# Another fixed order for the attention and gate stages of a fused attention and mixture kernel

## The chip, the cores and the metric

The kernel runs on one core of a Trainium2 chip. The metric is device time in microseconds (us) of one execution; the runs of a kernel are given with their median. The engines are TensorE (PE in the rows, with PEld for its weight loads), VectorE (DVE), ScalarE (ACT), GpSimd (POOL) and SyncE (SP), which issues the DMAs here. Each engine works its own queue in order.

## The reference

Attention over 2 batches, 8 heads, 576 positions of width 64: a softmax over the keys within 3 positions, plus a softmax of averaged queries on averaged keys (factor 4) whose result is repeated four times. Its output is a matrix of 1152 tokens by 512. A gated layer and a mixture of eight experts follow:

```python
def _moe_ref(x, w_gate, w_val, w_out):
    g = x @ w_gate
    silu = g * (1.0 / (1.0 + np.exp(-g)))
    val = x @ w_val
    return silu * val @ w_out

def _moe2_ref(x, w_gate, w1, w2):
    logits = x @ w_gate
    P = np.exp(logits - logits.max())
    for _ in range(8):                      # rows and columns in turn
        ...
    for e in range(E):
        h = np.maximum(x @ w1[e], 0.0)
        out += P[:, e:e + 1] * (h @ w2[e])
```

## The kernel before, in words

Matrices are split into a high and a low half of 16 bits, so that a product is three matmuls for each block of depth (mm3, L219). The program has three stages: attention together with the preparation of the gate weights, the gate products, and from the output products on the experts. The first two follow one table, PLAN, which is read from left to right; each entry is a step and the number of its pair of heads (0 to 7) or of its block of 128 gate columns (0 to 11, in hexadecimal). Inside them every engine's queue keeps the order in which the table issued its instructions. Behind the bar in PLAN the attention's PSUM banks are closed and the late gate products begin. Behind the table stands act_split, and then a scheduler orders the rest.

Steps of a pair of heads: K, Q, Z and W are loads. kd and qd add four positions (DVE, or POOL through qt: qe L492, qd L499). s0, s1 and s2 are scores (TensorE), m0 to m2 their maxima (DVE L536, L537), e0 to e2 exponentials with sums (ACT). r makes the reciprocals of the sums (DVE L557, L558), and ha and hb multiply by them (POOL L563, L568, tile ex), so ha and hb wait for r. px, py and pv add values (POOL L504, L508, L515, tiles vt and vdz, or DVE L513 alone). t are transposes and c their copies (ACT), o the products with the values, w and j the join (ACT, DVE L625), u and l the high and low half of the result (ACT, DVE L639, tile xhl).

Steps of a gate block: gR is its load, ga to gd its conversion from 64 bits (gb L247 or L245, gB L250, gc L253, gd L256, all DVE; ga ACT), ge its maximum (ACT L286), gp and gq or a POOL reduction spread it, gm makes the scale, gh and gl the two halves (ACT L306, DVE L310). Blocks 0 to 2 have their first 512 tokens multiplied early (y0, y1, with ya to yd behind them); all other products are late ones: zp is the product for the gate, zs its SiLU (ACT L692), zq the product for the value, zv their product (DVE L694), zj its maximum. The first digit of a z step is the chunk of tokens, 0 for the first 512 and 1 for the other 640. Late products share two PSUM pairs: the third product waits until the first one's SiLU has read its pair. Steps beginning with w prepare the output weights. sa, sg, sb and sp split the gate result of chunk 0 into halves (ACT L211, DVE L212, three blocks to an sp), in the order in which the blocks' zp steps stood; the output products (TensorE, tile wo) of chunk 0 start behind them and read blocks 0 to 11 in that order, into the same two PSUM pairs.

FILL gives a number of products that nobody reads, of a constant tile (L131, tile warm), to be issued into a bank ahead of a step's own products.

Of the kernel before, what the change touches and what calls it, by code (L numbers as in the profile page):

```python
# [56 lines left out]
PLAN = """
K0 Q0 K1 Q1 K2 Q2 Z0 W0 W1 Z1 W2 kd0 qd0 s00 kd1 s10 m00 s20 e00 m10 qe1 s01 m20 K3 Q3 e10 qd1 kd2 W3
s11 m01 e20 qd2 s21 s02 e01 m11 K4 Q4 r0 gR0 m21 s12 ha0 e11 m02 pv1 s22 hb0 e02 m12 t0 pv0 e21 m22 c0
r1 kd3 e12 ha1 o0 qe3 e22 xg0 pv2 Z2 K5 w0 hb1 Q5 kd4 gR1 qd3 s03 j0 W4 qe4 r2 t1 xm0 m03 ha2 s13 e03  # L60
qd4 xp0 m13 s23 hb2 c1 xr0 xu0 ga0 o1 m23 u0 kd5 e13 t2 gb0 Z3 K6 l0 Q6 qe5 c2 pv3 W5 s04 w1 gB0 e23 s14
qd5 j1 gc0 u1 s24 ga1 o2 r3 m04 px4 m14 e04 ha3 m24 gd0 w2 e14 hb3 j2 ge0 l1 t3 qe6 kd6 e24 s05 gR2 W6
gb1 c3 Z4 qd6 gp0 K7 r4 s15 Q7 py4 gq0 m05 u2 W7 ha4 gm0 o3 e05 m15 l2 s25 gh0 pv4 pv5 hb4 e15 m25 t4
gl0 w3 e25 s06 px6 j3 c4 py6 s16 r5 gB1 ga2 ha5 m06 o4 kd7 u3 hb5 m16 e06 s26 gc1 t5 w4 e16 qe7 m26 xg1
j4 c5 pv6 gd1 s07 e26 px7 xm1 s17 ge1 l3 qd7 m07 xp1 py7 r6 gR3 gp1 e07 m17 s27 Z5 ha6 Z6 xr1 gq1 y00
xu1 e17 hb6 m27 gb2 tu0 u4 gm1 t6 gB2 ya0 l4 gh1 y10 yb0 c6 gc2 gl1 e27 o5 gd2 ga3 y01 pv7 r7 w5 ge2 yc0
ha7 j5 gR4 gb3 u5 gp2 Z7 hb7 y11 yd0 ya1 gq2 tl0 lb0 yj0 gm2 yb1 gh2 gB3 t7 yc1 gl2 o6 c7 yd1 y02 gc3 w6
ga4 l5 yj1 j6 o7 ya2 gd3 u6 y12 yb2 ge3 l6 gb4 w7 gR5 yc2 j7 gp3 yd2 u7 gB4 yj2 l7 gq3 gc4 | zp10 gm3
gd4 gh3 ge4 gl3 zp12 zs10 gq4 gR6 ga5 gm4 gh4 gb5 zq10 zs12 gB5 gl4 gc5 zq12 zv10 ga6 gd5 zj10 gb6 ge5
zp14 zv12 gq5 gR7 gB6 zj12 gm5 gc6 gh5 zp04 gd6 zs14 gl5 ge6 zp11 zs04 gq6 wR0 ga7 gm6 gh6 gb7 zp03 zs11  # L70
gl6 gB7 gc7 zp16 zs03 gd7 wa0 wb0 ge7 wB0 zq11 zs16 wc0 gq7 gR8 gm7 wd0 zq03 we0 zv11 gh7 wm0 wR1 zj11
zp06 gl7 wh0 zv03 ga8 wl0 zp05 zj03 gb8 zs06 gB8 wa1 zq14 gc8 zs05 wb1 gd8 wB1 ge8 zp13 zv14 wc1 gq8 gR9
zj14 gm8 wd1 gh8 zq04 zs13 gl8 we1 zp15 zv04 wR2 wm1 zj04 ga9 wh1 zp08 gb9 zs15 wl1 gB9 zp17 zs08 gc9
wa2 gd9 wb2 ge9 zq13 wB2 wc2 zs17 gq9 gRa wd2 zq17 gm9 we2 zv13 gh9 wm2 wR3 zj13 gl9 zq15 wh2 zv17 gaa
wl2 zj17 gba zp09 zv15 wa3 gBa zq05 zj15 gca zs09 wb3 gda zp19 zv05 gea wB3 zj05 wc3 gqa gRb gma zq16
zs19 wd3 gha we3 gla zp07 zv16 wR4 wm3 zj16 wh3 zq09 zs07 wl3 gab zp18 gbb wa4 zv09 gBb zj09 wb4 zp0a
gcb zs18 wB4 gdb zq18 zs0a wc4 geb wd4 gqb wR5 we4 gmb zq07 zv18 ghb wm4 zj18 glb zq0a wh4 zv07 wl4 zj07
wa5 zq06 zv0a wb5 zj0a wB5 zp0b wc5 zv06 wd5 zj06 zp1a zs0b we5 wm5 wh5 zq19 zs1a wl5 zq0b zv19 zj19
zq08 zv0b zj0b zp1b zv08 zj08 sa0 sg0 zq1a zs1b sb0 sp0 zq1b sp1 zv1a sp2 zj1a zv1b sp3 zj1b
"""  # L80
# [951 lines left out]
```

## Time and profile before

| what | value |
|---|---|
| median of 3 runs | 1006.35 us (1005.7 to 1007.02) |
| the profiled execution | 1003.09 us, span 1001.3 us |
| TensorE busy | 987.3 us, 99% of the span |
| DVE busy | 752.3 us, 75% |
| ACT busy | 439.0 us, 44% |
| POOL busy | 61.7 us, 6% |
| the start of the output products | 216.08 us |

The share of busy time is a mean over stages with different limits. A row of a timeline gives its start, its duration, engine, source line, operation and tiles (out<-in), and in brackets the idle time of the engine ahead of it with what ended it. The end of a matmul is modelled, so a busy TensorE is not one at its peak.

### The profile page before, as it was taken

How to read it: one execution, taken by the hardware profiler on the slowest of the kernel's cores; microseconds unless marked ns; L12 is line 12 of the kernel's file. 1: busy time of each engine (PE TensorE's matmuls, PEld its weight loads, DVE VectorE, ACT ScalarE, POOL GpSimd, SP SyncE). 2: the span in 40 equal slices, each digit the busy share in tenths (PEclk: the TensorE clock that was granted, in tenths of full speed). 3: DMA queues.
4: the chain of work that ended last, by engine and by line, in shares of the span. 5: the costliest groups of instructions: out<-in, count | busy, mean ns of one | idle time of the engine just before them, and what ended most of it. 6: DMA issues, size and time to landing. Idle time of an engine off the chain costs nothing.

```text
span 1001.3 us, 16401 instructions
## 1 busy us (share of the span) xinstructions
PE 987.3 (99%) x6592; PEld 619.3 (62%) x6596; DVE 752.3 (75%) x1532; ACT 439.0 (44%) x913; POOL 61.7 (6%) x80
## 2 busy tenths in 40 slices
...
GB/s 306 225 113 140 149 114 159 126 1 1 85 1 2 85 84 43 43 89 39 43 56 72 1 43 89 39 43 49 79 1 43 84 44 43 42 44 1 1 43 52
DMA packets 12987, 67.95 MB, mean 68 GB/s; under 512 B 1456, under 2 KB 1840, under 8 KB 6512
## 3 DMA queue, kind: packets, MB, share of 16 engines
...
q8 instruction: 51, 0.84, 0.4%
...
## 4 chain that ended last, share of the span: by engine, by line
PE 90%; DVE 7%; ACT 1%; DMA 1%; issue 1%; DVEq 0%; ACTq 0%
PE y L219 37%; PE p L219 32%; PE gv L219 11%; PE wo L219 7%; DMA v<-in_vd 1%; DVE s L536 1%; DVE xhl L639 1%; DVE cvg L256 1%; DVE cvg L253 1%; DVE ahl L212 0%; PE lt L748 0%; DVE x L625 0%; PE pw L131 0%; ACT ex L547 0%; DVE vdz L513 0%
## 5 line engine op out<-in xcount | busy, mean ns | idle before, releaser
L219 PE MATMUL y<-w,hhl 128*128 128x512 f16 (+1 forms) x1752 | 395.7, 376 | 0.0
L219 PE MATMUL p<-bop,w 128*128 128x320 f16 (+1 forms) x2688 | 353.5, 286 | 0.6 <-ACT s L917 0.4
L219 PEld LDWEIGHTS <-w 128*128 128x128 f16 x2688 | 262.9, 98 | 90.3 <-issue 2.0
L219 PEld LDWEIGHTS <-hhl 128*128 128x128 f16 x1752 | 171.5, 98 | 178.9
L928 ACT ACTIVATE hhl<-h 128x640 f16<-128x640 f32 (+1 forms) x128 | 82.7, 675 | 158.6 <-DVE h L900 158.6
L219 PE MATMUL gv<-xhl,gv 128*128 128x320 f16 (+1 forms) x864 | 142.1, 326 | 2.8 <-ACT act L692 1.1
L959 DVE SCALAR_TENSOR_TENSOR acc<-y,pe,acc 128x512 f32<-128x512 f32 (+1 forms) x64 | 47.3, 740 | 101.3 <-PE y L219 100.5
L211 ACT ACTIVATE w<-r,s_w 128x256 f16<-128x256 f32 (+1 forms) x96 | 71.2, 783 | 117.7 <-PE y L219 86.3
L219 PEld LDWEIGHTS <-gv 128*128 128x128 f16 x864 | 84.1, 98 | 58.8 <-issue 3.6
L929 DVE SCALAR_TENSOR_TENSOR hhl<-h,hhl 128x640 f16<-128x640 f32 (+1 forms) x128 | 93.9, 753 | 17.4 <-ACT hhl L928 16.4
L900 DVE SCALAR_TENSOR_TENSOR h<-p,u 128x256 f32<-128x256 f32 (+1 forms) x192 | 84.8, 452 | 19.4 <-PE p L219 13.9
L212 DVE SCALAR_TENSOR_TENSOR w<-r,s_w,w 128x256 f16<-128x256 f32 (+1 forms) x96 | 78.2, 834 | 16.8 <-ACT w L211 16.7
L219 PE MATMUL wo<-ahl,wo 128*128 128x320 f16 (+1 forms) x408 | 70.0, 326 | 0.0
L219 PEld LDWEIGHTS <-wo 128*128 128x128 f16 x432 | 42.0, 98 | 30.3 <-issue 1.7
L900 DVE SCALAR_TENSOR_TENSOR u<-p,u 128x320 f32<-128x320 f32 (+1 forms) x128 | 57.5, 449 | 4.2 <-PE p L219 3.4
L211 ACT ACTIVATE w<-cmb,s_w 128x512 f16<-128x512 f32 x64 | 43.0, 710 | 37.0 <-DVE cmb L384 35.0
L917 ACT ACTIVATE s<-p 128x256 f32<-128x256 f32 (+1 forms) x64 | 25.4, 396 | 54.9 <-PE p L219 54.8
L187 DVE TENSOR_REDUCE mxw<-r 128x1 f32<-128x1024 f32 x32 | 37.4, 1213 | 14.2 <-DMA r<-in_w 14.2
L212 DVE SCALAR_TENSOR_TENSOR w<-cmb,s_w,w 128x512 f16<-128x512 f32 x64 | 46.3, 743 | 0.0
L404 ACT ACTIVATE j<-r 128x1024 f16<-128x1024 f32 x32 | 33.5, 1047 | 26.9 <-DMA r<-in_w 24.1
...
L900 DVE SCALAR_TENSOR_TENSOR u<-p,s 128x256 f32<-128x256 f32 (+1 forms) x64 | 28.9, 451 | 3.9 <-PE p L219 3.9
...
## 6 DMA issues: line engine op xcount, KB each, us to landing
...
```

The source lines that it names most:

```text
L187: V.tensor_reduce(o, i, axis=axis, op=ALU.max, apply_absolute_value=True)
L211: return (A.activation(hi, src, AF.Copy, scale=s), V.scalar_tensor_tensor(lo, src, s, hi, op0=ALU.mult, op1=ALU.subtract))
L212: V.scalar_tensor_tensor(lo, src, s, hi, op0=ALU.mult, op1=ALU.subtract))
L219: T.matmul(ps, lhsT=wf(i, k), rhs=xf(j, k), start=n == 0, stop=n == 3 * nk - 1)
L253: V.scalar_tensor_tensor(o, hi, 0xC0000000, o, op0=ALU.bitwise_and, op1=ALU.bitwise_or)
L256: V.scalar_tensor_tensor(o, lo, 29, o, op0=ALU.logical_shift_right, op1=ALU.bitwise_or)
L404: A.activation(junk, t[:, 2 * j:2 * j + 2].rearrange("p a n -> p (a n)"), AF.Abs, accum_out=mx[:, 2 * i + j:2 * i + j + 1])
L900: V.scalar_tensor_tensor(o, ps, HSC, u, op0=ALU.mult, op1=ALU.add)
L917: A.activation(s1, p1, AF.Copy, scale=HSC)
L928: ra = A.activation(t[:, 0], h, AF.Relu)
L929: rv = V.scalar_tensor_tensor(t[:, 1], h, 0.0, t[:, 0], op0=ALU.max, op1=ALU.subtract)
L959: V.scalar_tensor_tensor(acc[t][:, ds], ps, p[:, t:t + 1], acc[t][:, ds], op0=ALU.mult, op1=ALU.add)
```

## The change

PLAN is another permutation of the same 562 steps, with the bar at the same place (305 steps ahead of it), and FILL has other numbers, 25 in sum where it had 21.

```diff
-FILL = {"s00": 3, "o0": 2, "o1": 1, "t3": 12, "t4": 3}
+FILL = {"s00": 3, "o0": 8, "t3": 8, "t4": 6}
 PLAN = """
...
-r1 kd3 e12 ha1 o0 qe3 e22 xg0 pv2 Z2 K5 w0 hb1 Q5 kd4 gR1 qd3 s03 j0 W4 qe4 r2 t1 xm0 m03 ha2 s13 e03
+m22 r1 e12 qe3 o0 ha1 e22 xg0 kd4 Z2 K5 qd3 pv2 w0 Q5 hb1 gR1 s03 r2 W4 qe4 j0 t1 xm0 m03 ha2 xp0 e03
...
```

The late products stand in this order before, zp10 zp12 zq10 zq12 zp14 zp04 zp11 zp03 zp16 zq11 zq03 zp06 zp05 zq14 zp13 zq04 zp15 zp08 zp17, and in this order now, zp10 zp12 zp11 zq12 zp14 zq10 zp04 zp03 zq14 zq03 zp06 zp16 zq11 zp05 zp13 zp17 zq04; the last three are zp1b zq1a zq1b in both. Block 6 is first read by zp16 before and by zp06 now, block 7 by zp17 in both. The reduction pv0 on DVE stood behind m12 and now stands ahead of m21.

POOL's queue from the addition of pair 4's values to the second share of pair 4. In the names, the digit behind ex, rs, qt, qd and vt is the pair. Before:

```order
L504 TENSOR_TENSOR vt4_619<-v44_415 72x256
L563 TENSOR_TENSOR ex3_448<-ex3_448,rs3_614 128x640
L568 TENSOR_TENSOR ex3_448<-ex3_448,rs3_614 96x432
L492 TENSOR_TENSOR qt6_673<-q6_541 128x576
L499 TENSOR_TENSOR qd6_698<-qt6_673 128x288
L508 TENSOR_TENSOR vt4_619<-v44_415 72x256
L563 TENSOR_TENSOR ex4_623<-ex4_623,rs4_704 128x640
L515 TENSOR_TENSOR vdz0_110<-vt4_619 72x256
L568 TENSOR_TENSOR ex4_623<-ex4_623,rs4_704 96x432
```

And of the changed kernel:

```order
L563 TENSOR_TENSOR ex3_449<-ex3_449,rs3_615 128x640
L568 TENSOR_TENSOR ex3_449<-ex3_449,rs3_615 96x432
L504 TENSOR_TENSOR vt4_670<-v44_420 72x256
L492 TENSOR_TENSOR qt6_685<-q6_561 128x576
L508 TENSOR_TENSOR vt4_670<-v44_420 72x256
L499 TENSOR_TENSOR qd6_727<-qt6_685 128x288
L515 TENSOR_TENSOR vdz0_110<-vt4_670 72x256
L563 TENSOR_TENSOR ex4_583<-ex4_583,rs4_742 128x640
L568 TENSOR_TENSOR ex4_583<-ex4_583,rs4_742 96x432
```

The first vt of pair 4 moved from ahead of the shares of pair 3 to behind them, the second one to ahead of qd6, and vdz0 to ahead of the shares of pair 4.

DVE's queue around the sums of pair 4 (rs4), which release ex4 on POOL, and the low half of pair 2 (xhl). Before:

```order
L557 TENSOR_REDUCE rs4_704<-sts0_112 128x16
L558 RECIPROCAL rs4_704<-rs4_704 128x16
L194 TENSOR_REDUCE gr_gv0_717<-sm0_700 128x1
L536 TENSOR_REDUCE s5_0_680<-s5_0_680 128x5
L537 TENSOR_SCALAR stb1_115<-s5_0_680 128x5
L180 TENSOR_SCALAR u_gv0_725<-gr_gv0_717 128x1
L181 TENSOR_SCALAR u_gv0_725<-u_gv0_725 128x1
L182 TENSOR_SCALAR s_gv0_726<-u_gv0_725 128x1
L183 TENSOR_SCALAR i_gv0_727<-u_gv0_725 128x1
L536 TENSOR_REDUCE s5_1_707<-s5_1_707 128x5
L537 TENSOR_SCALAR stb1_115<-s5_1_707 128x5
L639 SCALAR_TENSOR_TENSOR xhl_126<-x12_641,s_x10_476,xhl_126 128x512
```

And of the changed kernel:

```order
L536 TENSOR_REDUCE s5_0_674<-s5_0_674 128x5
L537 TENSOR_SCALAR stb1_115<-s5_0_674 128x5
L194 TENSOR_REDUCE gr_gv0_716<-sm0_697 128x1
L180 TENSOR_SCALAR u_gv0_718<-gr_gv0_716 128x1
L181 TENSOR_SCALAR u_gv0_718<-u_gv0_718 128x1
L182 TENSOR_SCALAR s_gv0_719<-u_gv0_718 128x1
L183 TENSOR_SCALAR i_gv0_720<-u_gv0_718 128x1
L536 TENSOR_REDUCE s5_1_701<-s5_1_701 128x5
L537 TENSOR_SCALAR stb1_115<-s5_1_701 128x5
L557 TENSOR_REDUCE rs4_742<-sts0_112 128x16
L558 RECIPROCAL rs4_742<-rs4_742 128x16
L639 SCALAR_TENSOR_TENSOR xhl_126<-x12_642,s_x10_470,xhl_126 128x512
```

The two rows of rs4 moved from the head of this piece to directly ahead of the L639.

DVE's queue at the end of the gate stage: ahl0 are the low halves of chunk 0 by block, act1_10 and act1_11 the L694 of blocks 10 and 11. Before:

```order
L212 SCALAR_TENSOR_TENSOR ahl0_0_2635<-act0_0_1014,sc0_2594,ahl0__2634 128x512
L212 SCALAR_TENSOR_TENSOR ahl0_1_2638<-act0_1_1132,sc0_2594,ahl0_0_2635 128x512
L212 SCALAR_TENSOR_TENSOR ahl0_2_2641<-act0_2_1250,sc0_2594,ahl0_1_2638 128x512
L212 SCALAR_TENSOR_TENSOR ahl0_4_2669<-act0_4_1553,sc0_2594,ahl0_2_2641 128x512
L212 SCALAR_TENSOR_TENSOR ahl0_3_2672<-act0_3_1619,sc0_2594,ahl0_4_2669 128x512
L212 SCALAR_TENSOR_TENSOR ahl0_6_2675<-act0_6_1744,sc0_2594,ahl0_3_2672 128x512
L694 SCALAR_TENSOR_TENSOR act1_10_2466<-gv1_10_1_2600,iv1_10_2464,act1_10_2466 128x640
L212 SCALAR_TENSOR_TENSOR ahl0_5_2679<-act0_5_1769,sc0_2594,ahl0_6_2675 128x512
L212 SCALAR_TENSOR_TENSOR ahl0_8_2682<-act0_8_1933,sc0_2594,ahl0_5_2679 128x512
L212 SCALAR_TENSOR_TENSOR ahl0_9_2685<-act0_9_2109,sc0_2594,ahl0_8_2682 128x512
```

And of the changed kernel:

```order
L212 SCALAR_TENSOR_TENSOR ahl0_0_2639<-act0_0_1028,sc0_2598,ahl0__2638 128x512
L212 SCALAR_TENSOR_TENSOR ahl0_1_2642<-act0_1_1137,sc0_2598,ahl0_0_2639 128x512
L212 SCALAR_TENSOR_TENSOR ahl0_2_2645<-act0_2_1260,sc0_2598,ahl0_1_2642 128x512
L694 SCALAR_TENSOR_TENSOR act1_10_2468<-gv1_10_1_2602,iv1_10_2466,act1_10_2468 128x640
L212 SCALAR_TENSOR_TENSOR ahl0_4_2674<-act0_4_1587,sc0_2598,ahl0_2_2645 128x512
L212 SCALAR_TENSOR_TENSOR ahl0_3_2677<-act0_3_1623,sc0_2598,ahl0_4_2674 128x512
L212 SCALAR_TENSOR_TENSOR ahl0_6_2680<-act0_6_1706,sc0_2598,ahl0_3_2677 128x512
L694 SCALAR_TENSOR_TENSOR act1_11_2569<-gv1_11_1_2648,iv1_11_2567,act1_11_2569 128x640
L212 SCALAR_TENSOR_TENSOR ahl0_5_2686<-act0_5_1795,sc0_2598,ahl0_6_2680 128x512
L212 SCALAR_TENSOR_TENSOR ahl0_8_2689<-act0_8_2012,sc0_2598,ahl0_5_2686 128x512
```

The L694 of block 10 moved ahead of three L212, that of block 11 likewise, and block 7 is split ahead of block 9.

## Rows read from the trace of the kernel before

**Rows 1.** Windows: stretch, its length, busy us of PE, PEld, DVE, ACT, POOL, clock, DMA.
```profile
5.65:91.56 85.91, 78.95 (x879) 61.31 (x882) 83.21 (x180) 67.05 (x282) 43.36 (x38) 0.96 0.61 202
...
96.74:216.08 119.34, 118.50 (x744) 72.68 (x743) 98.22 (x177) 78.54 (x137) 3.33 (x8) 1.00 0.35 122
```

**Rows 2.** Timeline of PE, 88 to 217 us: start, us, engine, line, operation, idle before.
```profile
88.02 1.52 PE L219 MATMUL gv<-xhl,gv 128*128 128x320 f16 x10 [0.73 <-DVE x L625]
...
90.37 5.32 PE L219 MATMUL gv<-xhl,gv 128*128 128x320 f16 x38 [0.83 <-DVE xhl L639]
...
96.74 15.52 PE L219 MATMUL gv<-xhl,gv 128*128 128x320 f16 x106 [1.06 <-ACT act L692]
...
111.83 103.42 PE L219 MATMUL gv<-xhl,gv 128*128 128x320 f16 x640
...
216.08 0.39 PE L219 MATMUL wo<-ahl__2634,wo 128*128 128x512 f16 x1 [0.84 <-DVE act L694]
```

**Rows 3.** Timeline of DVE and of ACT around 92 to 97 us.
```profile
92.19 1.22 DVE L256 SCALAR_TENSOR_TENSOR cvg<-rawg,cvg 128x1024 uint32<-128x1024 uint32 x1
...
95.90 0.79 ACT L692 ACTIVATE act<-gv,iv 128x640 f32<-128x640 f32 x1
```

**Rows 4.** Timeline of DVE: rows of L639, L256 and L253 up to 70 us.
```profile
30.64 1.90 DVE L639 SCALAR_TENSOR_TENSOR xhl<-x,s_x,xhl 128x512 f16<-128x512 f32 x1
...
39.10 2.97 DVE L256 SCALAR_TENSOR_TENSOR cvg<-rawg,cvg 128x1024 uint32<-128x1024 uint32 x1
...
42.79 1.05 DVE L639 SCALAR_TENSOR_TENSOR xhl<-x,s_x,xhl 128x512 f16<-128x512 f32 x1
...
47.25 1.75 DVE L639 SCALAR_TENSOR_TENSOR xhl<-x,s_x,xhl 128x512 f16<-128x512 f32 x1
...
56.24 2.65 DVE L253 SCALAR_TENSOR_TENSOR cvg<-rawg,cvg 128x1024 uint32<-128x1024 uint32 x1
...
61.93 1.31 DVE L639 SCALAR_TENSOR_TENSOR xhl<-x,s_x,xhl 128x512 f16<-128x512 f32 x1
...
68.69 0.81 DVE L639 SCALAR_TENSOR_TENSOR xhl<-x,s_x,xhl 128x576 f16<-128x576 f32 x1
...
69.82 1.22 DVE L253 SCALAR_TENSOR_TENSOR cvg<-rawg,cvg 128x1024 uint32<-128x1024 uint32 x1
```

**Rows 5.** Timeline of POOL: one row of each kind, and those of 38 to 46 us.
```profile
27.89 0.67 POOL L499 TENSOR_TENSOR qd<-qt 128x288 f32<-128x288 f32 x1
...
38.72 0.90 POOL L568 TENSOR_TENSOR ex<-ex,rs 96x432 f32<-96x432 f32 x1
...
39.59 1.40 POOL L492 TENSOR_TENSOR qt<-q 128x576 f32<-128x576 f32 x1
...
41.06 1.53 POOL L499 TENSOR_TENSOR qd<-qt 128x288 f32<-128x288 f32 x1
...
42.56 0.73 POOL L508 TENSOR_TENSOR vt<-v 72x256 f32<-72x256 f32 x1
...
45.64 1.26 POOL L563 TENSOR_TENSOR ex<-ex,rs 128x640 f32<-128x640 f32 x1 [2.34 <-DVE gr_gv L194]
```

**Rows 6.** Timeline of PE at 35.59 us; windows ahead of and at half clock.
```profile
35.59 2.76 PE L131 MATMUL t<-warm 128*128 128x512 bf16 x11
...
41.40:44.40 3.00, 1.19 (x11) 1.04 (x11) 3.00 (x6) 2.23 (x9) 1.90 (x2) 1.00 0.13 16
...
44.50:51.30 6.80, 6.58 (x65) 5.33 (x66) 6.63 (x16) 6.01 (x27) 3.90 (x5) 0.50 0.93 322
```

**Rows 7.** Timelines of DVE, ACT and PE at the end of the gate stage.
```profile
211.05 4.18 DVE L212 SCALAR_TENSOR_TENSOR ahl<-act,sc,ahl 128x512 f16<-128x512 f32 x5
...
215.15 0.88 DVE L694 SCALAR_TENSOR_TENSOR act<-gv,iv,act 128x640 f32<-128x640 f32 x1
...
208.76 0.79 ACT L692 ACTIVATE act<-gv,iv 128x640 f32<-128x640 f32 x1 [1.69 <-PE gv L219]
...
216.74 4.26 PE L219 MATMUL wo<-ahl,wo 128*128 128x512 f16 x19
```

More of the change, by code (lines that the diff above doesn't have):

```diff
@@ L55 @@
 PVV = (0, 1, 2, 3, 5)
-FILL = {"s00": 3, "o0": 2, "o1": 1, "t3": 12, "t4": 3}
+FILL = {"s00": 3, "o0": 8, "t3": 8, "t4": 6}
 PLAN = """
-K0 Q0 K1 Q1 K2 Q2 Z0 W0 W1 Z1 W2 kd0 qd0 s00 kd1 s10 m00 s20 e00 m10 qe1 s01 m20 K3 Q3 e10 qd1 kd2 W3
-s11 m01 e20 qd2 s21 s02 e01 m11 K4 Q4 r0 gR0 m21 s12 ha0 e11 m02 pv1 s22 hb0 e02 m12 t0 pv0 e21 m22 c0
-r1 kd3 e12 ha1 o0 qe3 e22 xg0 pv2 Z2 K5 w0 hb1 Q5 kd4 gR1 qd3 s03 j0 W4 qe4 r2 t1 xm0 m03 ha2 s13 e03
-qd4 xp0 m13 s23 hb2 c1 xr0 xu0 ga0 o1 m23 u0 kd5 e13 t2 gb0 Z3 K6 l0 Q6 qe5 c2 pv3 W5 s04 w1 gB0 e23 s14
@@ L62 @@
[L62 to L76, printed above, removed]
@@ L77 @@
-gcb zs18 wB4 gdb zq18 zs0a wc4 geb wd4 gqb wR5 we4 gmb zq07 zv18 ghb wm4 zj18 glb zq0a wh4 zv07 wl4 zj07
-wa5 zq06 zv0a wb5 zj0a wB5 zp0b wc5 zv06 wd5 zj06 zp1a zs0b we5 wm5 wh5 zq19 zs1a wl5 zq0b zv19 zj19
-zq08 zv0b zj0b zp1b zv08 zj08 sa0 sg0 zq1a zs1b sb0 sp0 zq1b sp1 zv1a sp2 zj1a zv1b sp3 zj1b
+K0 Q0 K1 Q1 K2 Q2 Z0 W0 W1 Z1 W2 kd0 qd0 s00 kd1 s10 m00 s20 e00 m10 qe1 s01 K3 m20 Q3 e10 qd1 kd2 W3
+s11 m01 e20 qd2 s21 s02 e01 m11 K4 Q4 r0 gR0 pv0 s12 ha0 e11 m21 s22 hb0 m02 e21 pv1 t0 e02 m12 kd3 c0
@@ new lines @@
+m22 r1 e12 qe3 o0 ha1 e22 xg0 kd4 Z2 K5 qd3 pv2 w0 Q5 hb1 gR1 s03 r2 W4 qe4 j0 t1 xm0 m03 ha2 xp0 e03
+s13 xr0 qd4 xu0 hb2 c1 s23 m13 m23 u0 t2 ga0 kd5 o1 l0 c2 gb0 s04 qe5 e13 Z3 pv3 K6 Q6 gB0 W5 w1 e23 s14
+qd5 m04 gc0 e04 o2 r3 j1 ga1 ha3 s24 m14 u1 gd0 w2 e14 hb3 j2 l1 ge0 t3 px4 kd6 s05 u2 gb1 gR2 qe6 m24
+c3 W6 Z4 gp0 m05 s15 K7 e24 py4 Q7 gq0 gm0 W7 qd6 s25 e05 m15 pv4 r4 o3 l2 gh0 ha4 m25 pv5 e15 hb4 gl0
+w3 t4 e25 px6 j3 s06 ga2 py6 r5 c4 gB1 s16 ha5 m06 u3 kd7 o4 e06 hb5 m16 gc1 s26 w4 e16 t5 pv6 j4 qe7
```

15 lines of the change are left out of this document (added).

## The prediction

> **What bounds the kernel now.** I read the busy times by stage first [rows 1]. Up to 91.56 us the vector engine (DVE) is the limit: in 85.91 us it is busy 83.21, while TensorE's 78.95 holds unread products and work at half clock. From 96.74 us TensorE is the limit: 118.50 busy of 119.34 up to 216.08, where the output products start; 1001.3 - 216.08 = 785 us follow. Second, TensorE in order of time [rows 2], where a bracket is an idle stretch and what ended it. It waits 0.73, 0.83 and 1.06 us around 88 to 97 us, then runs 640 products without a hole from 111.83 to 215.25, waits 0.84 for an L694 on DVE, and starts the output products at 216.08. So the end moves only if one of two dates moves: 96.74, when the gate products begin to run without a hole, or 216.08.
>
> Third, what sets 96.74 [rows 3]. DVE ends its L256 for block 4 at 92.19 + 1.22 = 93.41; ScalarE then takes that block's maximum, loads a table, and runs the SiLU of the first late product at 95.90 to 96.69, which frees the PSUM pair for the third late product. That chain hangs on the running total of DVE's queue. Fourth, where DVE's rows are longer than their kind [rows 4]: L639 takes 0.81 for 576 columns undisturbed, but 1.90, 1.05, 1.75 and 1.31 for 512; L256 takes 1.22 [rows 3] and once 2.97; L253 takes 1.22 and once 2.65. Where POOL (GpSimd) is shown beside them [rows 5], each long one stands over its rows. The excess is 1.09 + 0.24 + 0.94 + 0.50 + 1.75 + 1.43 = 5.95 us of DVE's 83.
>
> **The change part by part.** Order alone moves, and from act_split on all five queues hold the same rows, so the 785 us behind 216.08 cost the same.
>
> *DVE's load ahead of the late products: 0.* The block 4 L256 is the 193rd row of DVE's queue in both programs, and the rows ahead of it are the same ones in another order. Without collisions and waits they take the same sum, so 96.74 moves only by what collisions and new waits do.
>
> *Collisions on DVE.* I place the new neighbours by hand, with clean durations [rows 5]: the shares ex 1.26 and 0.90, qt 1.40, vt and vdz (as large) 0.73, qd 0.67. (a) L639 for pair 0 now stands ahead of gb0, so gb0 rather than L639 meets qt5: bounds 0 and 1.09, taken 1.09, the row it replaces. (b) gd0 (L256) stands 0.7 us earlier in DVE's sum and POOL has ex3, ex3, vt4, qt6, vt4, qd6 in one run. Handed over at the first boundary it costs about 0; if POOL keeps the port through the run, 0.90 + 0.73 + 1.40 + 0.73 + 0.67 = 4.43. Taken 0.90 + 0.73 = 1.63, since the row of before waited over a rest and one whole row (38.72 + 0.90 = 39.62 passed, then qt to 40.99). (c) The next L639 follows on qt6 and vt4: 0 to 1.3, taken 0.9 (before 0.24). (d) The L639 for pair 2 now follows r4 directly. r4 releases ex4, which before started at 45.64, after r4, with the L639 only at 47.25. Now DVE asks first: 0 to 0.94, taken 0. (e) gl0 comes when the two vt of pair 6 can run: 0 to 1.46, taken 0.4. (f) L253 for block 1 meets a vdz in place of a qt: it meets the rest of an ex row, put at 0.2, and then 0.73 alone or 0.73 + 1.40: 0.2 to 2.33, taken 0.93 (before 1.43). (g) gd1 and the next L639, 0.5 before: taken 0.8. Sum 1.09 + 1.63 + 0.9 + 0 + 0.4 + 0.93 + 0.8 = 5.75 against 5.95: **-0.2 us**. At the lower bounds about 1.2 stays, a gain of 4.7; at the upper ones, with c and d at 0, it is 1.09 + 4.43 + 1.46 + 2.33 + 0.8 = 10.1, a loss of 4.2.
>
> A gain there is capped: for some 40 us ahead of 88 TensorE is itself all but full, so it can come forward little beyond its own waits, 0.73 + 0.83 + 1.06 = 2.62.
>
> Which way a boundary between two POOL rows goes is what decides here. gd0 asked at 39.10, let an ex end at 39.62 and a qt run to 40.99, and then got in ahead of qd6, which took 1.53 where clean it takes 0.67 [rows 5]. The Trainium skill, "SBUF — State Buffer", section "Who interferes with whom", says that the port pair DVE shares with GpSimd is an exclusive lock: who issues first holds it for the whole instruction, the other fully blocks. The trace agrees that one side blocks, but a wait across two instructions, as gd0's 2.97 is, does not follow from it. By the page gd0 would pay only ex3's rest; what that would do is the first rival, in this kernel's own rows.
>
> *The unread products: 0.* FILL goes from 21 to 25. Eight of them stand ahead of o0, where TensorE sits until ScalarE's copy is there; t3 loses four in a stretch where it waits for POOL anyway; t4 gets three more, 3 x 0.25 = 0.75 us if the eleven products of 2.76 us [rows 6] are the measure, 1.5 at half clock. That is covered by the 2.62 of waits before 96.74; with that cover gone it would be paid. The granted clock is 0.50, 1.2 GHz, from 44.5 to 51.3 after a stretch with TensorE busy 1.19 of 3.00 us [rows 6], and the new order keeps the level product of block 0 behind the same maximum, so I expect the drop again. It cost nothing before: DVE had 6.63 busy of 6.80 there.
>
> *The first 30 us: 0.* The reduction vdz0 moves ahead of block m21, so ScalarE's e21 starts up to 0.8 us later, and o0 behind it. DVE has other rows in that time; its next row that needs e21, the sums of pair 1, comes some 4 us later. Bounds 0 and +0.8.
>
> *The gate stage: 0.* A product needs its block's weights ready and its PSUM pair read. In 640 products of before there is no hole [rows 2]. Block 6's first product moves from the ninth of the late ones to the eleventh, so it has more time; block 7's from the nineteenth to the sixteenth, three products of up to 3.24 us less. No bound but 0 below; above, I leave 1 us.
>
> *The end of the gate stage: -0.8.* TensorE's first output product needs the PSUM pair that the L694 of block 10 frees. That row ran at 215.15 to 216.03 [rows 7], behind six L212. The two products behind TensorE's end of 208.76 take (215.25 - 208.76) / 2 = 3.24 each, so its own product had ended at 212.0. Now it stands behind three L212, at about 212.7. TensorE is then free to go at 215.25 + 0.04: 216.08 - 215.29 = **0.79**. What is late next: the L212. They run at (4.18 - 0.75) / 4 = 0.86 each and pass two L694 of 0.8, and the last, block 11, comes at about 222.3. Matmuls of an output product come (4.26 - 0.38) / 18 = 0.216 apart, three to a block, so from 215.29 block 11's rest is read after 34 of them, at 222.6. The margin is 0.3 us; if it fails, the gain shrinks by as much.
>
> **Sum:** -0.2 - 0.8 = -1.0 us. The profiled run took 1003.09 us with a span of 1001.3; that becomes 1002.1. The median of the runs is 1006.35, 3.26 above the profiled one, and the same difference gives **1005.4 us**. About 0.2%, 2 us, is what a measurement can tell from no change.
>
> **The rivals.** *First: POOL hands over at the first boundary.* Then gd0 costs about 0 and the collisions shrink by up to 4.7; the cap of 2.62 and the tail's 0.8 give 1006.35 - 3.4 = 1002.9. For it: qd6 had to give way. Against: gd0's wait past 39.62. I give it 28%.
>
> *Second, slower: POOL keeps the port for a whole run.* Its place is gd0: ex3 to qd6 without a gap, 4.43 us, then gl0 and L253 alike. DVE loses 4.2, the tail returns 0.8: 1006.35 + 3.4 = 1009.7. It decides from a loss on DVE of 2.8. For it: gd0 lost a boundary though it had asked half a us ahead. Against: it got in at the second. 17%.
>
> *Third: the tail's wait only moves.* The L212 of the last blocks arrive too late and TensorE waits inside the first output product: 1006.1. 5%.
>
> **How the numbers follow.** The forecast has 50%: of that 44 within 0.2%, 3 on each side for waits I have not seen. With the first rival 28 + 3 = 31% faster, with the second 17 + 3 = 20% slower, and 44 + 5 = 49% the same. The range takes in both rivals' prices but for their far edges: 1002.7 to 1009.5. The likeliest case's own range is 1004.4 to 1006.4.
>
> **What would show it.** The tail: no TensorE wait at the first output product, and L694 of block 10 near 213. The collisions: the sum of excesses of L639, L253, L256, gb0 and gl0 near 5.8; gd0 near 2.9 us; the pair-2 L639 near 0.8. The 640-odd gate products without a hole from about 96.5. I am wrong if the date of the block 4 L256 moves by over 2 us, if a wait over 0.5 us shows inside the gate stage, or if the clock falls twice and TensorE, not DVE, sets that date.

## The result, and the profile after

The changed kernel takes **1010.56 us** (median of 11 runs, 1008.24 to 1017.5) where the kernel before took 1003.25 beside it (11 runs, 1001.87 to 1007.02): a ratio of **1.0064**, 95% interval 1.0043 to 1.0084. It is slower; 1005.4 was forecast, with a range up to 1009.5. A ratio here is the one on record for all runs of both kernels; the quotient of the two medians, 1.0073 for this one, can lie some 0.2% off it. One execution of all those below, 1477.47 us at a mean clock of 0.654 in the run with kd4 behind gR1, counts in none of that run's figures.

The profiled execution took 1014.45 us, span 1012.6, which is 3.9 us above its kernel's median; that of before took 1003.09 and 1001.3. Its mean granted clock is 0.988, before 0.996. Since the clock has two levels here, the time at 1.2 GHz is about twice the missing share of the span: 2 x 0.012 x 1012.6 = 24 us, before 8.

First the stages, which answer to [rows 1]. The columns are the same; the last row is a stretch of before up to the start of the L256 for block 4.

```profile
5.65:91.56 85.91, 76.17 (x787) 62.78 (x786) 72.28 (x160) 59.94 (x267) 41.88 (x37) 0.86 0.58 189
5.65:104.51 98.86, 87.31 (x885) 68.73 (x884) 85.12 (x185) 67.47 (x282) 42.26 (x38) 0.88 0.54 175
54.20:78.10 23.90, 23.51 (x161) 21.84 (x162) 15.19 (x41) 13.70 (x61) 11.55 (x12) 0.50 0.21 73
109.07:227.40 118.33, 118.33 (x744) 72.78 (x744) 97.68 (x176) 78.54 (x136) 4.53 (x8) 1.00 0.36 123
```

```profile
5.65:92.19 86.54, 79.58 (x884) 61.76 (x887) 83.77 (x186) 67.05 (x282) 43.36 (x38) 0.96 0.60 200
```

VectorE (third busy column) is no longer full: 72.28 of 85.91 us, where it had 83.21 in [rows 1]. The clock column says 0.86 for that stage, and 0.50 for all of 54.20 to 78.10, in which TensorE is busy 23.51 of 23.90 us and VectorE only 15.19. For that stretch TensorE is the limit, at half its speed. The second row ends where VectorE begins the L256 for block 4, the date that the prediction watches. It moved from 92.19 to 104.51, by 12.32 us: VectorE works 85.12 - 83.77 = 1.35 longer, and idles 13.74 us instead of 2.77, so 10.97 more. The loss is idle time.

What VectorE waited for up to that date, in the view of waits (engine, tile and line, what ended the wait: us in all, times, longest):

```profile
DVE mxv L454 <- PE vv L449: 3.1, 1, 3.1
DVE kd L485 <- DMA k<-in_kT: 2.6, 1, 2.6
DVE gr_v L194 <- PE sv L190: 1.3, 1, 1.3
DVE s L536 <- PE s L525: 1.3, 2, 0.9
DVE gr_gv L194 <- PE sm L190: 1.1, 1, 1.1
DVE x L625 <- ACT avd L616: 0.9, 1, 0.9
DVE s L536 <- PE s L529: 0.5, 1, 0.5
DVE gv L310 <- ACT gv L306: 0.5, 1, 0.5
```

One wait of 2.6 us is for a load, the keys of pair 4:

```profile
24.03 0.75 DVE L485 TENSOR_REDUCE kd<-k 128x144 f32<-128x576 f32 x1 [2.58 <-DMA k<-in_kT]
```

TensorE ends 3.1 + 1.3 + 1.3 + 1.1 + 0.5 = 7.3 us of the others, all of them between 58 and 76 us, in the slow stretch. Before, the same view of VectorE has 0.9 us in all.

TensorE, GpSimd and VectorE where the slow stretch begins, which answers to [rows 5, 6], and after them the same two products of TensorE before:

```profile
44.10 1.22 PE L525 MATMUL s<-k,q 128*128 128x64 f32 x10
...
47.42 1.47 PE L131 MATMUL t<-warm 128*128 128x512 bf16 x6
51.19 0.77 PE L576 MATMUL t<-ident,ex 128*128 128x128 f32 x5 [2.30 <-POOL ex L563]
54.59 1.17 PE L580 MATMUL t<-ident,ex 96*72 96x96 f32 x6 [2.64 <-POOL ex L568]
55.83 2.23 PE L525 MATMUL s<-k,q 128*128 128x64 f32 x10
...
49.59 1.55 POOL L563 TENSOR_TENSOR ex<-ex,rs 128x640 f32<-128x640 f32 x1 [2.68 <-DVE rs L558]
51.09 3.44 POOL L568 TENSOR_TENSOR ex<-ex,rs 96x432 f32<-96x432 f32 x1
...
49.36 0.66 DVE L639 SCALAR_TENSOR_TENSOR xhl<-x,s_x,xhl 128x512 f16<-128x512 f32 x1
50.65 1.93 DVE L513 TENSOR_REDUCE vdz<-v 72x256 f32<-72x1024 f32 x1
52.49 1.28 DVE L310 SCALAR_TENSOR_TENSOR gv<-cvg,s_gv,gv 128x1024 f16<-128x1024 f32 x1
54.86 2.88 DVE L250 TENSOR_SCALAR cvg<-cvg 128x1024 uint32<-128x1024 uint32 x1
```

```profile
50.64 1.04 PE L576 MATMUL t<-ident,ex 128*128 128x128 f32 x5
51.52 0.66 PE L580 MATMUL t<-ident,ex 96*72 96x96 f32 x6
```

Behind the six unread products TensorE idles 2.30 us for the first share of pair 4 and, 0.77 us of work later, 2.64 for the second; before, it waited for neither. From 54.2 on its rows are nearly double: ten products of a score take 2.23 us, where they took 1.22 at 44.10. The first share starts at 49.59, before at 45.64 [rows 5], since the sums that release it stand behind the maxima now. The second takes 3.44 us; a row of its form took 0.90 in [rows 5].

The rows of VectorE that answer to [rows 4], where they are longer than the clean 0.81 (L639), 0.68 (L247) and 1.22 (L256), and the GpSimd rows that the L250 above lets pass:

```profile
32.13 0.87 DVE L639 SCALAR_TENSOR_TENSOR xhl<-x,s_x,xhl 128x512 f16<-128x512 f32 x1
33.17 0.91 DVE L247 TENSOR_SCALAR cvg<-cvg 128x1024 f32<-128x1024 f32 x1 [0.17 <-ACT cvg L241]
...
39.92 1.23 DVE L256 SCALAR_TENSOR_TENSOR cvg<-rawg,cvg 128x1024 uint32<-128x1024 uint32 x1
...
41.86 2.66 DVE L639 SCALAR_TENSOR_TENSOR xhl<-x,s_x,xhl 128x512 f16<-128x512 f32 x1
...
45.11 1.19 DVE L247 TENSOR_SCALAR cvg<-cvg 128x1024 f32<-128x1024 f32 x1
...
65.23 1.63 DVE L256 SCALAR_TENSOR_TENSOR cvg<-rawg,cvg 128x1024 uint32<-128x1024 uint32 x1
...
86.93 1.83 DVE L247 TENSOR_SCALAR cvg<-cvg 128x1024 f32<-128x1024 f32 x1
...
54.50 0.74 POOL L504 TENSOR_TENSOR vt<-v 72x256 f32<-72x256 f32 x1
55.20 0.73 POOL L508 TENSOR_TENSOR vt<-v 72x256 f32<-72x256 f32 x1
55.90 1.25 POOL L563 TENSOR_TENSOR ex<-ex,rs 128x640 f32<-128x640 f32 x1
```

The excess lies at other places than before, and is about as large (worked out below).

The end of the two stages, which answers to [rows 2, 3, 7]:

```profile
104.51 1.21 DVE L256 SCALAR_TENSOR_TENSOR cvg<-rawg,cvg 128x1024 uint32<-128x1024 uint32 x1
...
108.22 0.80 ACT L692 ACTIVATE act<-gv,iv 128x640 f32<-128x640 f32 x1
...
109.07 118.50 PE L219 MATMUL gv<-xhl,gv 128*128 128x320 f16 x744 [0.15 <-ACT act L692]
227.40 0.38 PE L219 MATMUL wo<-ahl__2638,wo 128*128 128x512 f16 x1
...
224.90 0.88 DVE L694 SCALAR_TENSOR_TENSOR act<-gv,iv,act 128x640 f32<-128x640 f32 x1
```

From that L256 to the first product without a hole the chain is as long as before, 109.07 - 104.51 = 4.56 (before 96.74 - 92.19 = 4.55). The output products start at 227.40, without the wait of 0.84: 11.32 us later than 216.08, which is the whole loss of this execution (1014.45 - 1003.09 = 11.36). The medians differ by less, 1010.56 - 1003.25 = 7.31.

### The profile page after: what moved, and what is told of

It reads as the page before. It is cut to its first block, busy times and chain, and to the rows that moved or that the text cites. A ratio compares the mean times of both kernels' runs of the same rounds, so it can differ in the third digit from the quotient of the medians.

```text
span 1012.6 us, 16413 instructions
## 1 busy us (share of the span) xinstructions
PE 995.8 (98%) x6600; PEld 627.0 (62%) x6600; DVE 753.8 (74%) x1532; ACT 440.7 (44%) x913; POOL 61.8 (6%) x80
## 4 chain that ended last, share of the span: by engine, by line
PE 92%; DVE 5%; ACT 1%; DMA 1%; issue 1%; POOL 0%; ACTq 0%; DVEq 0%
PE y L219 37%; PE p L219 32%; PE gv L219 12%; PE wo L219 7%; DMA k<-in_kT 1%; PE s L525 1%; DVE xhl L639 0%; PE lt L748 0%; DVE x L625 0%; DVE s L536 0%; PE pw L131 0%; PE s L529 0%; DVE vdz L513 0%; DVE cvg L247 0%; POOL ex L568 0%
## 5 line engine op out<-in xcount | busy, mean ns | idle before, releaser
L212 DVE SCALAR_TENSOR_TENSOR w<-r,s_w,w 128x256 f16<-128x256 f32 (+1 forms) x96 | 78.1, 832 | 16.8 <-ACT w L211 16.7
L212 DVE SCALAR_TENSOR_TENSOR w<-cmb,s_w,w 128x512 f16<-128x512 f32 x64 | 46.2, 739 | 0.0
```

The lines of the kernel that those rows point to most:

```text
L212: V.scalar_tensor_tensor(lo, src, s, hi, op0=ALU.mult, op1=ALU.subtract))
```

## The experiments

All ratios are to the kernel before, run beside the variant on the same chip, with the 95% interval. Medians of before were 1006.24, 1004.97, 1005.95 and 1005.43 us in the four groups of runs, 120 runs in all. The change itself was timed in a group of its own, with 1003.25 for before, and was not run again beside the variants; the nearest to it there is the new table with the old numbers, 1.0052.

The theory: pair 4's shares come late, TensorE idles, the clock falls, and VectorE waits for a TensorE at half speed; VectorE's wait for a load adds to it. The rivals: the numbers of unread products are the loss, or VectorE's own lateness and collisions are.

**Table or unread products.** FILL and PLAN crossed.

```diff
 plan_new_fill_old: the new PLAN
-FILL = {"s00": 3, "o0": 8, "t3": 8, "t4": 6}
+FILL = {"s00": 3, "o0": 2, "o1": 1, "t3": 12, "t4": 3}
 plan_old_fill_new: the PLAN of before
-FILL = {"s00": 3, "o0": 2, "o1": 1, "t3": 12, "t4": 3}
+FILL = {"s00": 3, "o0": 8, "t3": 8, "t4": 6}
```

> The new table with the numbers of unread products of before (o0 2, o1 1, t3 12, t4 3). By the theory of the clock (pair 4's shares come late on POOL, TensorE idles twice at pair 4's transposes and values, and the granted clock falls to 0.50 for over 20 us) nothing is mended, since only three unread products stand ahead of t4: half clock for 15 to 30 us and 1008 to 1016 us. By the theory that the new numbers of unread products are the loss: about 1003 us, as before. By the theory that the collisions of VectorE and GpSimd are the loss: as the change, 1008 to 1011.

> The table of before with the new numbers of unread products. By the theory of the clock the shares of pair 4 come early as before, so the half clock stays short, 0 to 8 us, and the time within 1002 to 1005 us. By the theory of the unread products: it carries the loss, 1008 us or more.

Measured: 1010.91 us, 1.0052 (1.0034 to 1.0070), and 1005.34 us, 0.9996 (0.9981 to 1.0011). The table carries the loss. But the second one's profile has 17 us at half clock (54 to 71 us) where 0 to 8 were expected: the order of before also loses the clock in some executions.

**The idle filled.** 24 unread products ahead of pair 4's transposes in the changed kernel.

```diff
-FILL = {"s00": 3, "o0": 8, "t3": 8, "t4": 6}
+FILL = {"s00": 3, "o0": 8, "t3": 8, "t4": 24}
```

> The changed kernel with 24 unread products ahead of t4 where it has 6: they fill TensorE's 2.30 us of idle ahead of that step's own products and hide nothing of VectorE's lateness. By the theory of the clock the granted clock holds or falls for at most 8 us, and the time is 1002 to 1006 us: most of the 11 us of the profiled loss come back. By the theory that VectorE's own lateness (2.58 us waited for the load of pair 4's keys, 2.88 us of gB1) is the loss, the date at which the gate products run without a hole moves by under 2 us and the time stays at 1008 or more.

Measured: 1008.26 us, 1.0027 (1.0005 to 1.0050). TensorE's rows there:

```profile
48.69 5.35 PE L131 MATMUL t<-warm 128*128 128x512 bf16 x24
53.88 0.71 PE L576 MATMUL t<-ident,ex 128*128 128x128 f32 x5
55.87 0.69 PE L580 MATMUL t<-ident,ex 96*72 96x96 f32 x6 [1.28 <-POOL ex L568]
```

The products cost more TensorE time than the 2.30 they replace and release nothing, and still the ratio is 1.0027 for 1.0064, with a median of the mean clock of 0.995 for 0.990. The two intervals overlap, so that over half of the loss is gone is likely and not shown; that the clock came back speaks for the idle as what brought it down. The rest is not the clock's. Two of the seven executions had a mean clock of 1.00 and took 1005.73 and 1005.88 us; the six of before at 1.00 took 1002.22 to 1004.24. The wait for pair 4's keys was 3.42 us in this profile, and the 18 products add at most 18 x 0.216 - 2.30 = 1.6. The time is the one that the second theory expected, the clock the one of the first: both hold a part.

**The load.** kd4, first behind pv2, then behind gR1.

```diff
 new_kd4_back
-... e22 xg0 kd4 Z2 K5 qd3 pv2 w0 Q5 hb1 gR1 s03 ...
+... e22 xg0 Z2 K5 qd3 pv2 kd4 w0 Q5 hb1 gR1 s03 ...
 new_kd4_far
+... e22 xg0 Z2 K5 qd3 pv2 w0 Q5 hb1 gR1 kd4 s03 ...
```

> The changed kernel with one step put back: kd4 behind pv2, so that VectorE does not wait for the load of pair 4's keys with that reduction behind it. By the theory that VectorE's lateness is the loss: 2 to 2.6 us come back, 1007 to 1008, with the half clock as it was. By the theory of the clock: pair 4's shares come 2 us earlier but TensorE still idles at t4, so the half clock shortens or stays, 15 to 24 us, and the time is 1006 to 1011; if the clock should hold, it is 1003 or less.

> The changed kernel with kd4 alone put back, behind gR1. If the wait for the load of pair 4's keys carries 2 to 2.6 us of the loss by itself: ratio to the kernel before 1.003 to 1.0045, with the idle stretches of 2.30 and 2.64 us at t4 as they were. If it carries nothing, since what VectorE gains there is waited out later: 1.005 to 1.008.

Measured: 1010.64 us, 1.0045 (1.0027 to 1.0062), and 1006.46 us, 1.0025 (1.0006 to 1.0043). Far enough back, this step alone has a ratio 0.4% under the change's; the two intervals just meet. The idle stretches at pair 4 stayed at 2.30 and 2.63 or 2.64 us in both, but the half clock behind them lasted 13.7 us in either profile and not 23.9, so its length does not follow from these two stretches alone.

**The held port.** Why does the second share take 3.44 us? One row moved on VectorE, or one on ScalarE:

```diff
 new_gl0_back
-... m25 pv5 e15 hb4 gl0 w3 t4 e25 ... c4 gB1 s16 ...
+... m25 pv5 e15 hb4 w3 t4 e25 ... c4 gB1 gl0 s16 ...
 new_gh0_late
-... o3 l2 gh0 ha4 m25 pv5 e15 hb4 gl0 ...
+... o3 l2 ha4 m25 pv5 e15 gh0 hb4 gl0 ...
```

> The changed kernel with one row moved: gl0 (L310 on VectorE) stands behind gB1 and no longer directly behind pv5 (L513). By the theory that GpSimd's second share of pair 4 takes 3.44 us instead of 0.90 because two VectorE rows without a gap (L513 1.93, L310 1.28) keep the port: it ends behind L513 alone, 2.2 to 2.5 us instead of 3.44, and TensorE's idle stretch ahead of L580 of pair 4 falls from 2.64 to 1.4 to 1.7 us; the time falls by 0 to 3 us, as the clock goes. By the rival, that this row is long for a reason of GpSimd's own (a fetch of instructions): it stays at 3.4.

> The changed kernel with one step moved, on ScalarE: gh0 (L306, the upper half of block 0) behind e15, so that the input of VectorE's L310 is ready later; VectorE's and GpSimd's own orders stay. By the theory that an L310 whose input is ready and that stands next behind the running row takes the port before it starts, L568 of pair 4 on GpSimd starts ahead of the end of L306 and takes 0.90 us (3.44 in the change), and the first GpSimd row that starts after the end of L306 is the long one instead; TensorE's 2.64 us ahead of L580 fall below 0.5. By the theory that L513 or the place of L310 in the queue blocks GpSimd: L568 stays above 3. The time: as with gl0 moved, ratio to the kernel before 1.002 to 1.004.

Measured: 1006.37 us, 1.0027 (1.0007 to 1.0046), and 1006.63 us, 1.0023 (1.0005 to 1.0040). The first missed its number: not 2.2 to 2.5 us but 0.90, with L513 beside it for its whole length. GpSimd and VectorE in that run:

```profile
51.09 0.90 POOL L568 TENSOR_TENSOR ex<-ex,rs 96x432 f32<-96x432 f32 x1
...
50.65 1.96 DVE L513 TENSOR_REDUCE vdz<-v 72x256 f32<-72x1024 f32 x1
52.52 0.74 DVE L625 TENSOR_TENSOR x<-o,avd 128x288 f32<-128x288 f32 x2
```

So L513 blocks nothing. What blocked the share is L310, though by their starts the two would not have met: the share would have ended at 51.09 + 0.90 = 51.99, and L310 started at 52.49. The second run says when. ScalarE, GpSimd and VectorE with gh0 late:

```profile
51.33 1.18 ACT L306 ACTIVATE gv<-cvg,s_gv 128x1024 f16<-128x1024 f32 x1
...
51.40 0.90 POOL L568 TENSOR_TENSOR ex<-ex,rs 96x432 f32<-96x432 f32 x1
52.27 0.74 POOL L504 TENSOR_TENSOR vt<-v 72x256 f32<-72x256 f32 x1
52.98 1.73 POOL L508 TENSOR_TENSOR vt<-v 72x256 f32<-72x256 f32 x1
...
50.95 1.97 DVE L513 TENSOR_REDUCE vdz<-v 72x256 f32<-72x1024 f32 x1
52.84 1.27 DVE L310 SCALAR_TENSOR_TENSOR gv<-cvg,s_gv,gv 128x1024 f16<-128x1024 f32 x1
```

L310's input is ready when L306 ends, at 52.51. The two GpSimd rows that began ahead of it take their 0.90 and 0.74; the one that began behind it, and 0.14 us behind L310's own start, takes 1.73 and ends 0.60 after L310. In the change L306 ended at 49.58 + 1.16 = 50.74, ahead of the share's 51.09: 51.09 + 3.44 = 54.53 is 0.76 after L310's end of 53.77.

These two runs also test the clock. In both, the second idle stretch ahead of pair 4's transposes is gone and the first one stays, 2.28 us with gl0 back and 2.29 with gh0 late. With gl0 back the clock held there and fell only at 56.8, in an idle stretch of 3.35 us, for 6.8 us. With gh0 late it fell at 52.7, after 1.2 us of work behind the first stretch, for 10.2 us:

```profile
53.32 2.23 PE L525 MATMUL s<-k,q 128*128 128x64 f32 x10
```

So one stretch of this length is at times enough to lose the clock, and at times not.

**Pair 4's steps early.** m24, e24, r4 and ha4 back, without and with kd4; and the two smallest repairs together.

```diff
 new_m24_early
-... m14 u1 gd0 w2 ... t3 px4 ... qe6 m24 ... gp0 m05 s15 K7 e24 ... W7 qd6 s25 e05 m15 pv4 r4 o3 l2 gh0 ha4 ...
+... m14 u1 m24 gd0 w2 ... t3 e24 px4 ... qe6 ... gp0 r4 m05 s15 K7 ... W7 qd6 ha4 s25 e05 m15 pv4 o3 l2 gh0 ...
 new_m24_kd4: the same, and
+... hb1 gR1 kd4 s03 ...
 new_kd4_gl0: the change, and
+... hb1 gR1 kd4 s03 ... c4 gB1 gl0 s16 ...
```

> The changed kernel with four steps put where they stood before relative to their neighbours: m24 ahead of gd0, e24 behind t3, r4 behind gp0, ha4 behind qd6. By the theory that the late shares of pair 4 make TensorE idle at t4 and so bring the low clock: the two idle stretches of 2.30 and 2.64 us shrink to under 0.8 each, half clock 4 to 14 us as in the kernel before, and 3 to 6 us of the loss come back; about 2.5 us, from the wait for the load of pair 4's keys, stay against the kernel before, ratio 1.002 to 1.003. By the theory that the order of VectorE with its collisions is the loss: ratio 1.005 or more.

> As the run with m24, e24, r4 and ha4 put back, and kd4 put back too, behind gR1, so that VectorE does not wait for the load of pair 4's keys. If the late shares and that wait are the two causes, nothing of the loss is left: ratio to the kernel before 0.998 to 1.001. If a third cause is there: 1.003 or more.

> The changed kernel with kd4 behind gR1 and gl0 behind gB1: the two repairs that are smallest, two steps of 562. If the wait for the keys' load and the held port are most of the loss: ratio 0.999 to 1.002. If pair 4's late sums (r4) matter beside the held port: 1.002 to 1.004.

Measured: 1004.94 us, 1.0017 (0.9996 to 1.0039); 1002.92 us, **0.9998** (0.9977 to 1.0020); 1006.35 us, 1.0012 (0.9996 to 1.0028). With five steps of 562 put back the loss is gone. TensorE at pair 4 in the first of these runs:

```profile
48.98 1.47 PE L131 MATMUL t<-warm 128*128 128x512 bf16 x5
50.28 0.71 PE L576 MATMUL t<-ident,ex 128*128 128x128 f32 x5
51.58 0.69 PE L580 MATMUL t<-ident,ex 96*72 96x96 f32 x6 [0.59 <-POOL ex L568]
```

Repairs beside the mean granted clock (median over each kernel's executions; 0.993 over the 120 of before). The last column takes the clock out as far as the runs allow: a straight line through the 120 runs of before falls by 0.56 us for each 0.001 of mean clock, and the column says by how much a kernel's runs lie above that line on average. Its standard errors are 0.2 to 0.7 us.

| kernel | ratio | clock | us above the line |
|---|---|---|---|
| the change | 1.0064 | 0.990 | 3.5 |
| the new table, old numbers | 1.0052 | 0.988 | 2.2 |
| pair 4's idle filled | 1.0027 | 0.995 | 4.1 |
| kd4 behind pv2 | 1.0045 | 0.989 | 2.5 |
| kd4 behind gR1 | 1.0025 | 0.993 | 0.9 |
| gl0 back, gh0 late | 1.0027, 1.0023 | 0.993 | 1.2, 1.0 |
| pair 4's steps early | 1.0017 | 0.994 | 0.4 |
| kd4 and gl0 | 1.0012 | 0.993 | 0.9 |
| kd4 and pair 4's steps | 0.9998 | 0.9945 | -0.8 |

Two parts of the loss come apart here. Filling the idle brings the clock back and leaves the distance from the line; the steps put back shorten that distance, and all of them but kd4 behind pv2 bring the clock back as well. So the clock carries a part of the loss, and another part stands at an equal clock. That this other part is the waits themselves is argued from the repairs, which take waits away and shorten it. The single repairs do not add up: 0.39% for kd4 and 0.37 for gl0, but 0.52 for both. With intervals of 0.2% to each side that is suggested rather than shown, and so is any order among them.

**The other way round.** Pair 4's steps late in the kernel before.

```diff
-... ha3 m24 gd0 ... kd6 e24 s05 gR2 W6 gb1 ... K7 r4 s15 ... W7 ha4 gm0 ... m15 l2 s25 gh0 pv4 pv5 hb4 e15 m25 t4 gl0 w3 ...
+... ha3 gd0 ... kd6 s05 gR2 W6 gb1 m24 ... K7 s15 e24 ... W7 gm0 ... m15 r4 l2 s25 gh0 pv4 ha4 m25 pv5 hb4 gl0 e15 t4 w3 ...
```

> The kernel before with pair 4's steps put as late as the change puts them: m24 behind gb1, e24 behind s15, r4 behind m15, ha4 behind pv4, and gl0 directly behind pv5. By the theory that the late shares of pair 4, with L310 of gl0 holding the port against the second one, make TensorE idle and bring the low clock: GpSimd's second share of pair 4 is long again (over 2 us, clean 0.90), TensorE idles 2 to 5 us ahead of pair 4's transposes, half clock rises by 5 us or more, and the time rises by 2 to 5 us, ratio 1.002 to 1.005. If these steps need the rest of the new order to do harm: ratio 0.999 to 1.001.

Measured: 1006.5 us, 1.0027 (1.0006 to 1.0048). TensorE idled 2.04 us ahead of pair 4's transposes, as expected, and by the ratio the time rose (the medians, 1006.5 and 1005.95, show hardly any of it); but the second share stayed at 0.90, because L306 ended at 52.67, behind its start of 52.28, and the next GpSimd row took 2.42 instead. The clock did not fall there in the profiled execution (it fell from 14 to 24 us, before these steps), so this run shows the price, not that the clock carries it.

**The tail, and a better version.**

```diff
 old_tail
-sa0 sg0 zq1a zs1b sb0 sp0 zq1b sp1 zv1a sp2 zj1a zv1b sp3 zj1b
+sa0 zq1a sg0 zs1b sb0 sp0 zq1b zv1a sp1 zj1a zv1b sp2 zj1b sp3
 best_c: old_tail, the new FILL, and
-... qd6 gp0 K7 r4 s15 Q7 py4 gq0 m05 u2 W7 ha4 gm0 o3 e05 m15 l2 s25 gh0 pv4 pv5 hb4 ...
+... qd6 K7 r4 s15 Q7 py4 m05 u2 W7 ha4 o3 e05 m15 l2 s25 gp0 pv4 pv5 gq0 gm0 gh0 hb4 ...
 best_a: new_m24_kd4, and
+... gR1 kd4 s03 xg0 ... t1 m03 xm0 ... s25 gp0 e05 m15 pv4 o3 l2 m25 gq0 gm0 pv5 gh0 ... c4 gB1 gl0 ...
 best_b: best_a, and
-FILL = {"s00": 3, "o0": 8, "t3": 8, "t4": 6}
+FILL = {"s00": 3, "o0": 8, "t3": 8, "t4": 8, "o4": 4}
+... s06 py6 r5 c4 ga2 gB1 gl0 ...
```

> The kernel before with the order of the last steps of the gate stage alone as in the change (sb0 sp0 zq1b zv1a sp1 zj1a zv1b sp2 zj1b sp3). By the prediction's step on the end of the gate stage: TensorE's idle of 0.83 or 0.84 us ahead of the first output product vanishes, no idle inside that product, minus 0.8 us (ratio 0.999, hardly to be told in the time, plain in the trace). By its third rival: TensorE waits inside the first output products instead, minus 0 to 0.3.

> The table of before with the new order of the last steps of the gate stage, the new numbers of unread products, and gp0, gq0, gm0 and gh0 back behind s25, so that TensorE's 1.81 us of idle ahead of the level product of block 0 goes. If that idle brings the drop of before: half clock 0 to 8 us, 2 to 4 us under the kernel before, ratio 0.996 to 0.998; if not, 0.999 (the 0.8 us of the tail alone).

> The run with m24, e24, r4, ha4 and kd4 put back, and three stalls more taken away: xg0 behind s03 with m03 ahead of xm0 (TensorE waited 1.54 us for a load of values), gp0, gq0, gm0 and gh0 back behind s25 (TensorE waited 2.50 us for the maximum of block 0), gl0 behind gB1. If idle stretches of TensorE bring the low clock, half clock falls to 0 to 8 us and the time is 2 to 4 us under the kernel before, ratio 0.996 to 0.998. If the idle goes elsewhere: 0.999 to 1.001.

> As best_a, with ga2 behind c4 on ScalarE (o4 waited 2.8 to 3.4 us for pair 4's copies in two runs), 8 unread products ahead of t4 for 6, and 4 ahead of o4. Same test: half clock 0 to 8 us, ratio 0.996 to 0.998, and not above best_a; if the unread products are on the path, 0.5 to 1.5 us above best_a.

Measured: old_tail 1004.94 us, 0.9990 (0.9973 to 1.0007); best_c 1004.04, 0.9991 (0.9974 to 1.0008); best_a 1008.24, 1.0043 (1.0022 to 1.0063); best_b 1008.51, 1.0033 (1.0011 to 1.0056). The tail does in the old order what the prediction says: its output products start at 218.03 without the wait of 0.83 or 0.84, and no idle stands in the first of them; the time cannot tell 0.8 us. best_c lands on the second of its two values, 0.999: without the 1.81 us of idle its profile still has 20.4 us at half clock, so that idle is not what the clock needs to fall. best_a and best_b miss. In best_a a longer stall stands in the place of those that were taken away, and TensorE's waits up to 110 us come to 12 us where the run that it builds on had 7.7:

```profile
57.10 1.34 PE L607 MATMUL o<-at,vz 64*64 64x60 f32 x40 [4.88 <-ACT at L586]
```

No version was shown to beat the kernel before.

## Why the prediction was wrong

**What bounds the kernel now: right for that execution, not for the kernel.** The chain from VectorE's load to 96.74 held to 0.01 us. But "It cost nothing before", said of the half clock, holds at most for that execution. In the runs of before that accompany the experiments, the six with a mean clock of 1.00 have a median of 1002.6 us, the 30 at 0.991 or below 1007.1. Time at half clock goes with a longer time before too, some 0.28 us for each us over 120 runs, though these runs alone do not say which of the two brings the other. The table of before with the new numbers, profiled with 17 us at half clock for 6.8, started its output products at 221.64 for 216.08. The 3.26 us by which the profiled execution stood under its median, which the prediction only carried along, lies within this spread. In the eleven runs beside the change the median of before is 1003.25, so those 3.26 us entered the forecast as an accident of three runs.

**The unread products: 0, with the drop of the clock in it: the first step that failed.** The prediction expected the drop of before again, at a price of nothing, and had no term for new idle of TensorE. The drop ahead of block 0's level product did not come; that product ran at 43.68 without a wait. And the three more unread products ahead of t4 were never the point. The idle behind them grew from nothing to 2.30 and 2.64 us, and the half clock from 6.8 to 23.9 us. With pair 4's steps early again the ratio falls to 1.0017, and with kd4 back as well to 0.9998.

The clock is a part of the price of this idle. In the 11 runs of the change time and mean clock go together, 1008.24 us at 0.993 and 1017.5 at 0.983. But at an equal clock the change is slower too: 1008.24 to 1009.47 in its three runs at 0.992 and 0.993, against 1006.5, the median of 41 runs of before there, and 1009.94 to 1011.25 in its three at 0.990, against 1005.87 to 1008.2 in five of before. As an estimate from the table above, the fall of the median clock from 0.993 to 0.990 is worth 3 x 0.56 = 1.7 us, and 3.5 us stand beside it. The split is rough: the runs of before are from other groups, and those beside the change, faster at 1003.25, have no clock on record.

**Collisions: -0.2: the sum near by luck, the other side left out.** On VectorE, over 0.81, 0.68, 1.22 and, for L250, 0.63, the excess is 0.06 + 0.23 + 1.85 + 0.51 + 2.25 + 0.41 + 1.15 = 6.46 us against 5.75 forecast. But the places that the prediction priced at 5.75 cost 0.06 + 0.23 + 1.85 + 0.41 = 2.55, and only one of its prices, (d), came out: (a) cost 0.23 for 1.09, (b) 0 for 1.63, (c) 1.85 for 0.9 and above its bound of 1.3, (e) and (f) nothing, (g) 0.41 for 0.8. The other 3.91 are the L250 at 54.86 and two L247, which it had not seen. gd0 cost nothing: it went in ahead of ex3's second half (39.92, 1.23), as the first rival has it, and L250 passed three GpSimd rows, as the second has it; neither decided. The L639 of pair 2 came through in 0.66, as point (d) says, which also shows that the 0.81 of 576 columns is too long for a clean row of 512. What (d) gained on VectorE, TensorE paid: the sums that moved to directly ahead of it are what the shares wait for, and the shares are what pair 4's transposes wait for. The prediction showed both queues in its own rows and asked only what VectorE loses.

**The first 30 us: 0, bounds 0 and +0.8: failed.** kd4 moved ahead of pv2 and waited 2.58 us for its load, with pv2 and all of VectorE behind it. Only ScalarE's e21 was considered there. This is the second step that failed: 2.58 us of waiting on VectorE where the sum has nothing. In the time it is only suggested: with pair 4's steps early the ratio is 1.0017 with kd4 where the change has it and 0.9998 with kd4 back, and the intervals overlap.

**The gate stage: 0, and its end, -0.8: right.** 744 products without a hole, and 118.33 us where before took 119.34: 1.0 less, 0.84 of it the wait.

**Rivals.** None of the three is what happened. The sentence on what would make it wrong names it nearly: the date moved by 12.3 us and TensorE set it, though the clock fell once and long, not twice.

**What stays open.** What makes the clock fall behind one idle stretch and not behind another of the same length, how long it then stays down, and why in some executions of either order it falls as early as 14 or 20 us. How the 1.35 us of VectorE's additional busy time come about: row by row its durations sum to only 0.4 us more than before. And why best_b is slower than the kernel before, at a median clock of 0.993 and with about as little idle of TensorE up to 110 us (8.0 us, before 7.4).
